# Transposing the second heads' probabilities on the vector engine, with an exchange through DRAM

## The chip, the core and the metric

The kernel runs on one core of a Trainium2 chip. Such a core has a tensor engine (PE) for matrix products and transposes, a vector engine (DVE), a scalar engine (ACT), GpSimd (POOL), and SyncE (SP), which here issues the DMA transfers. The engines run beside each other and wait for each other by semaphores. The measure is device time in microseconds, the median of several runs; lower is better. Times inside the kernel come from one profiled execution.

## The reference

For each of 8 batches and 8 heads, 576 queries attend to 576 keys of 64 numbers. Only the 32 largest scores of a row count. A low-rank mixer over the sequence and a two-layer MLP follow. All is in 32-bit floats.

```python
scores = scale * np.matmul(q, k.transpose(0, 1, 3, 2))          # (8, 8, 576, 576)
kth = np.partition(scores, -32, axis=-1)[..., -32:-31]
scores = np.where(scores >= kth, scores, -1e9)
attn = np.exp(scores - np.max(scores, axis=-1, keepdims=True))
attn = attn / (np.sum(attn, axis=-1, keepdims=True) + 1e-09)
x = np.matmul(attn, v)                                           # heads side by side: (8, 576, 512)
h = x.transpose(0, 2, 1) @ U @ V                                 # rank 32, over the sequence
u = x + h.transpose(0, 2, 1)
out = u + np.maximum(u @ w_ch1, 0.0) @ w_ch2                     # 512 -> 2048 -> 512
```

## The kernel before

Two heads of one batch form a *group*: 32 groups in all, four to a batch. A group has five *steps* (`CH = NT + 1`): t = 0 to 3 take 128 queries of both heads each, t = 4 takes the last 64 queries of both heads in one tile of 128 rows. So there are 160 steps, numbered n = 5 g + t, and the 31st is step 30, the first of group 6. The products of a step are spread over several turns of the main loop: in turn n the scores of step n + 1 are computed, the largest 32 of step n are found, step n - 1 is weighted (masked and put through the exponential), and the values of step n - 2 are taken.

The selection is DVE work: four rounds of MAX8, which finds the 8 largest of a row, with MATCH_REPLACE8 between them, which strikes them out. `front` is a generator, and each `yield` ends a piece that the main loop places among other work. Of a two-head step, head 1 is masked on POOL (`pooled`), head 0 on ACT and POOL (`gaps`):

```python
    def front(g, t):

        if t == 0:
            dens[g] = small.tile([P, 2 * NT + 1], F32, tag="den", name="den", bufs=3)
        chunks, den = S2s.pop((g, t)), dens[g]
        n = len(chunks)
        E2 = attn.tile([P, 2 * S], F32, tag="E", name="E", bufs=3)
        Es = [E2[:, c * S : (c + 1) * S] for c in range(n)]
        sums = [den[:, 2 * t + c : 2 * t + c + 1] for c in range(n)]
        probs[g, t] = E2
        curs, ms = list(chunks), [None] * n
        first = small.tile([P, 2, 8], F32, tag="first", name="first", bufs=3)
        nmax = small.tile([P, 2], F32, tag="nmax", name="nmax", bufs=4)
        order = (1, 0) if n == 2 else (0,)
        for c in order:
            ms[c] = first[:, c]
            nc.vector.max(ms[c], curs[c])
        yield
        early, pooled, gaps = ways(g, t)
        for i in range(1, TOPK // 8):
            if i == 1:
                nc.scalar.mul(nmax[:, 0:n], first[:, 0:n, 0], -SCALE)
                for c in early:
                    weigh(chunks[c], Es[c], nmax[:, c : c + 1])
            for c in order:
                nxt = attn.tile([P, S], F32, tag="rr", name="rr", bufs=3)
                nc.vector.match_replace(nxt, ms[c], curs[c], NEG)
                curs[c] = nxt
            for c in order:
                ms[c] = small.tile([P, 8], F32, tag="m8", name="m8", bufs=8)
                nc.vector.max(ms[c], curs[c])
            yield
        for c in pooled:
            nc.gpsimd.tensor_scalar(Es[c], chunks[c], ms[c][:, 7:8], NEG, ALU.is_lt, ALU.mult)
            nc.gpsimd.tensor_tensor(chunks[c], chunks[c], Es[c], ALU.add)
        for c in early:
            nc.vector.scalar_tensor_tensor(
                out=Es[c],
                in0=chunks[c],
                scalar=ms[c][:, 7:8],
                in1=Es[c],
                op0=ALU.is_ge,
                op1=ALU.mult,
                accum_out=sums[c],
            )
        if t == NT:
            del qkTs[g]
        yield
        for c in gaps:
            least = small.tile([P, 1], F32, tag="least", name="least", bufs=3)
            nc.scalar.mul(least, ms[c][:, 7:8], WIDEN)
            nc.scalar.activation(Es[c], chunks[c], AF.Relu, bias=least, scale=-WIDEN)
            nc.gpsimd.tensor_tensor(chunks[c], chunks[c], Es[c], ALU.subtract)
            yield
        for c in order:
            if c not in early:
                weigh(chunks[c], Es[c], nmax[:, c : c + 1], sums[c])
        if t == NT and g != NPAIR - 1:
            nc.scalar.activation(den, den, AF.Identity, bias=eps)
        yield
```

The probabilities have queries along the partitions; the product with v needs keys there. `turns` does this on the PE, four transposes of 128x128 into one PSUM tile and one ACT copy for each head, and one transpose for the last 64 keys of both heads. `values` multiplies with v:

```python
    def turns(g, t):


        E2 = probs.pop((g, t))
        nh = 2 if t < NT else 1
        PT = attn.tile([P, 2 * NT + 1, P], F32, tag="PT", name="PT")
        PTs[g, t] = PT
        for h in range(nh):
            tp = ps_t.tile([P, NT, P], F32, tag="tp", name="tp")
            for j in range(NT):
                a = h * (S + TAIL) + j * P
                nc.tensor.transpose(tp[:, j, :], E2[:, a : a + P], ident)
            nc.scalar.copy(PT[:, NT * h : NT * h + NT], tp)
            yield
        tp = ps_t.tile([P, P], F32, tag="tp", name="tp")
        a = MAIN if nh == 2 else S - P
        nc.tensor.transpose(tp, E2[:, a : a + P], ident)
        nc.scalar.copy(PT[:, NT * nh], tp)
        yield

# in values(g, t), for a step of two heads:
        PT = PTs.pop((g, t))
        # ... cut
        nc.tensor.matmul(O, lhsT=vd, rhs=PT[:, 2 * NT], start=True, stop=False)
        for j in range(NT):
            for h in range(2):
                nc.tensor.matmul(
                    O[half(h)],
                    lhsT=va[:, h, j, :],
                    rhs=PT[:, NT * h + j],
                    start=False,
                    stop=(j == NT - 1),
                )
```

From group 5 on (`blocked`) the DVE already transposes one thing in 32x32 blocks: q and k of the next group, which small transfers load as blocks into the places where they will be needed. It is one instruction a group, in the turn of t = 1, after the selection:

```python
        if blocked(g):
            nc.vector.transpose(qkT.rearrange("p i n -> p (i n)"), raw.pop(g))
            yield
            return
```

The MLP of a batch runs as filler: `fill()` emits a measured amount of its matmuls between the pieces of the attention of the next batch. The amount is reduced (`EARLY`) up to turn 42, and cut for t = 4 (`SHORT`). The MLP of the last batch has no attention beside it. Its results have channels along the partitions, and `turned_back` transposes them for the output:

```python
    def turned_back(b, chunks, lo, c, oT):


        def run():
            tp = ps_t.tile([P, 3, P], F32, tag="tp", name="tp")
            for i, t in enumerate(chunks):
                n = rows(t)
                nc.tensor.transpose(tp[0:n, i, :], oT[:, OFF[t] - lo : OFF[t] - lo + n], ident)
            ob = mlpp.tile([P, 3, P], F32, tag="ob", name="ob", bufs=3)
            nc.scalar.copy(ob[:, 0:2], tp[:, 0:2, :])
            if NT in chunks:
                nc.scalar.copy(ob[0:TAIL, 2], tp[0:TAIL, 2, :])
            t, cs = chunks[0], slice(c * P, (c + 1) * P)
            nc.sync.dma_start(
                out[b, 0:MAIN, cs].rearrange("(p t) c -> p t c", t=NT)[:, t : t + 2, :],
                ob[:, 0:2],
            )
            if NT in chunks:
                nc.sync.dma_start(out[b, MAIN:S, cs], ob[0:TAIL, 2])

        return run
```

The body of the main loop from group 4 on. The order of PE, ACT, DVE and POOL instructions is the order in which they are written here; the transfers on SyncE are ordered by the compiler's scheduler.

```python
        ease = eased(*divmod(n - 1, CH))
# ... cut: the turns up to 19
        if ease:
            next(last, None)
        fill()
        next(turning, None)
        fill()
        next(turning, None)
        fill()
        next(turning, None)
        fill()
        if ease:
            next(last, None)
        if n - 2 >= ALONE:
            values(*divmod(n - 2, CH))
        if n + 1 < STEPS:
            scores(*divmod(n + 1, CH))
        next(here, None)
        next_params(1)
        if n - 2 >= ALONE and (n - 2) % CH == NT:
            mixing.append(mixed((n - 2) // CH, 5))
        fill()
        next(here, None)
        fill()
        if n <= STEPS:
            turning = turns(*divmod(n - 1, CH))
        fill()
        next(here, None)
        next(ready, None)
        if t in (1, 3):
            next_params(1)
        next(here, None)
        fill()
    while mixing or fillers:
        fill()
```

Of the kernel before, what the change touches and what calls it, by code (L numbers as in the profile page):

```python
# [8 lines left out]
F32 = mybir.dt.float32  # L9
# [17 lines left out]
def kernel(  # L27
# [28 lines left out]
    nc = tc.nc  # L56
    B, H, S, D = q.shape
# [8 lines left out]
    assert S == MAIN + TAIL and D == 64 and H % 2 == 0 and C == 512 and TOPK % 8 == 0  # L66
    NPAIR = H // 2
    NP = B * NPAIR
    SCALE = 1.0 / float(D) ** 0.5
    NV = 3  # L70

# [7 lines left out]
    attn = ctx.enter_context(tc.tile_pool(name="attn", bufs=2))  # L79
    small = ctx.enter_context(tc.tile_pool(name="small", bufs=8))  # L80
    mlpp = ctx.enter_context(tc.tile_pool(name="mlpp", bufs=2))
    ps_s = ctx.enter_context(tc.tile_pool(name="ps_s", bufs=2, space=bass.MemoryType.PSUM))
    ps_t = ctx.enter_context(tc.tile_pool(name="ps_t", bufs=2, space=bass.MemoryType.PSUM))
    ps_m = ctx.enter_context(tc.tile_pool(name="ps_m", bufs=2, space=bass.MemoryType.PSUM))
# [36 lines left out]
    def rows(t):  # L121
        return P if t < NT else TAIL
# [221 lines left out]
    def weigh(chunk, E, nmax, total=None):  # L344

        nc.scalar.activation(E, chunk, AF.Exp, bias=nmax, scale=SCALE, accum_out=total)  # L346

# [13 lines left out]
# [54 lines that stand above are left out]
            nc.scalar.activation(Es[c], chunks[c], AF.Relu, bias=least, scale=-WIDEN)  # L415
            nc.gpsimd.tensor_tensor(chunks[c], chunks[c], Es[c], ALU.subtract)  # L416
            yield
        for c in order:
            if c not in early:
                weigh(chunks[c], Es[c], nmax[:, c : c + 1], sums[c])  # L420
        if t == NT and g != NPAIR - 1:
            nc.scalar.activation(den, den, AF.Identity, bias=eps)
        yield

    def turns(g, t):


        E2 = probs.pop((g, t))
        nh = 2 if t < NT else 1
        PT = attn.tile([P, 2 * NT + 1, P], F32, tag="PT", name="PT")  # L430
        PTs[g, t] = PT
        for h in range(nh):
            tp = ps_t.tile([P, NT, P], F32, tag="tp", name="tp")
            for j in range(NT):
                a = h * (S + TAIL) + j * P
# [8 lines that stand above are left out]
# [7 lines left out]
    def values(g, t):  # L451

        PT = PTs.pop((g, t))
        va, vd, vt = (a[g % NV] for a in (vas, vds, vts))
        O = ps_t.tile([P, P], F32, tag="tp", name="O")
        if t == NT:
            den, x = dens[g], xs[g % 2]
            inverse(g, 2 * NT if g == NPAIR - 1 else 0, 2 * NT + 1)
            for j in range(NT + 1):
                nc.tensor.matmul(  # L460
                    O,
                    lhsT=PT[:, j],
                    rhs=va[:, :, j, :] if j < NT else vt,
                    start=(j == 0),
                    stop=(j == NT),
                )
            for h in range(2):
                nc.scalar.mul(x[half(h), NT, half(h)], O[half(h), half(h)], den[half(h), 2 * NT :])
            return
        nc.tensor.matmul(O, lhsT=vd, rhs=PT[:, 2 * NT], start=True, stop=False)  # L470
        for j in range(NT):
            for h in range(2):
                nc.tensor.matmul(  # L473
                    O[half(h)],
                    lhsT=va[:, h, j, :],
                    rhs=PT[:, NT * h + j],
                    start=False,
                    stop=(j == NT - 1),
                )
        if t == 0:  # L480
            XTs[g] = attn.tile([P, MAIN], F32, tag="XT", name="XT")
        nc.scalar.copy(XTs[g][:, cols(t)], O)  # L482
# [99 lines left out]
    def turned_back(b, chunks, lo, c, oT):  # L582


        def run():
            tp = ps_t.tile([P, 3, P], F32, tag="tp", name="tp")
            for i, t in enumerate(chunks):
                n = rows(t)
                nc.tensor.transpose(tp[0:n, i, :], oT[:, OFF[t] - lo : OFF[t] - lo + n], ident)  # L589
            ob = mlpp.tile([P, 3, P], F32, tag="ob", name="ob", bufs=3)  # L590
            nc.scalar.copy(ob[:, 0:2], tp[:, 0:2, :])
            if NT in chunks:
                nc.scalar.copy(ob[0:TAIL, 2], tp[0:TAIL, 2, :])
            t, cs = chunks[0], slice(c * P, (c + 1) * P)
            nc.sync.dma_start(
                out[b, 0:MAIN, cs].rearrange("(p t) c -> p t c", t=NT)[:, t : t + 2, :],
                ob[:, 0:2],
# [5 lines that stand above are left out]
# [1 line left out]
    MLP_WORK = 2 * NF * NC * S / C  # L604


    CH = NT + 1
    STEPS = NP * CH
    ALONE = NPAIR * CH


    SLOTS, SHORT, EARLY = 8, 0.65, 0.91
# [31 lines left out]
    for n in range(STEPS + 2):  # L644
# [44 lines left out]
        if n < ALONE:  # L689
# [3 lines that stand above are left out]
            if n >= 3:  # L693
                values(*divmod(n - 3, CH))
                if (n - 3) % CH == NT:
                    mixing.append(mixed((n - 3) // CH, 3))
            list(turning)
            fill()
            next(here)
            if t < NT:  # L700
# [3 lines that stand above are left out]
            next(here)  # L704
            next(last, None)
            fill()
            next(here)
            if t in (0, 1):
                next_params(1)
            next(here)  # L710
            fill()
            if n >= 1:
                turning = turns(*divmod(n - 1, CH))
            continue
        if ease:
            next(last, None)
        fill()
        next(turning, None)
        fill()
        next(turning, None)  # L720
        fill()
        next(turning, None)
        fill()
# [9 lines left out]
            mixing.append(mixed((n - 2) // CH, 5))  # L733
        fill()
        next(here, None)
        fill()
        if n <= STEPS:
            turning = turns(*divmod(n - 1, CH))
# [40 lines left out]
```

## Time and profile before

| what | value |
|---|---|
| time, median of 3 | 1819.66 us (1819.0 to 1819.68) |
| span of the profiled execution | 1816.5 us |
| PE busy, share of the span | 1715.5 us, 94% |
| DVE busy | 1498.8 us, 83% |
| ACT busy | 1084.2 us, 60% |
| POOL busy | 846.8 us, 47% |
| chain of work that ended last | PE 81%, DVE 14% |

Busy time is the time in which an engine executes an instruction, whether or not anything waits for it. The chain is followed back from the last instruction, at each step to what released it. A group of instructions is written as line, engine, operation, output and input tile, shapes and count; then busy time and mean time of one in ns; then the idle time of its engine just before, and who ended it. For matmuls the end is modelled and overlaps the next one, so that the distance between two starts, the pitch, is what one costs.

### The profile page before, as it was taken

How to read it: one execution, taken by the hardware profiler on the slowest of the kernel's cores; microseconds unless marked ns; L12 is line 12 of the kernel's file. 1: busy time of each engine (PE TensorE's matmuls, PEld its weight loads, DVE VectorE, ACT ScalarE, POOL GpSimd, SP SyncE). 2: the span in 40 equal slices, each digit the busy share in tenths (PEclk: the TensorE clock that was granted, in tenths of full speed). 3: DMA queues.
4: the chain of work that ended last, by engine and by line, in shares of the span. 5: the costliest groups of instructions: out<-in, count | busy, mean ns of one | idle time of the engine just before them, and what ended most of it. 6: DMA issues, size and time to landing. Idle time of an engine off the chain costs nothing.

```text
span 1816.5 us, 28753 instructions
## 1 busy us (share of the span) xinstructions
PE 1715.5 (94%) x10285; PEld 1293.7 (71%) x10285; DVE 1498.8 (83%) x2995; ACT 1084.2 (60%) x2797; POOL 846.8 (47%) x591
## 2 busy tenths in 40 slices
PE   4666889999999999999999999999999999999999
PEld 2444556787777877788777877788777877788677
DVE  7999998998898888988888889889888898884000
ACT  4777786666656566565666665565656656564111
POOL 4777577444444545535444444444344453543000
PEclk7688899999999999999999999999999999999999
DMA  3232231111100111111001111110011111000000
GB/s 100 79 90 85 68 89 47 32 21 33 21 22 22 21 27 21 32 25 30 17 20 25 24 30 21 32 25 22 19 18 31 21 33 21 8 8 7 6 15 12
DMA packets 193823, 58.21 MB, mean 32 GB/s; under 512 B 156432, under 2 KB 191504, under 8 KB 193680
## 3 DMA queue, kind: packets, MB, share of 16 engines
q1 hardware_dynamic: 192624, 56.11, 13.4%
q8 instruction: 81, 1.33, 0.3%
q14 instruction: 62, 0.51, 0.1%
q10 hardware_dynamic: 1056, 0.26, 0.1%
HBM read 46.89 MB, written 9.44 MB: 31 GB/s over the span
## 4 chain that ended last, share of the span: by engine, by line
PE 81%; DVE 14%; POOL 2%; ACT 1%; issue 1%; DMA 0%; SPq 0%; POOLq 0%; DVEq 0%; ACTq 0%
PE mm L542 26%; PE mm L561 26%; PE sc L328 7%; DVE rr L390 6%; PE O L473 6%; PE tp L436 6%; DVE m L394 5%; DVE first L380 2%; PE sc L315 2%; PE O L460 2%; PE O L470 2%; PE up L517 1%; PE tp L589 1%; PE up L519 1%; PE tp L494 1%
## 5 line engine op out<-in xcount | busy, mean ns | idle before, releaser
L394 DVE MAX8 m<-rr 128x8 f32<-128x576 f32 x864 | 614.9, 749 | 5.5
L561 PE MATMUL mm<-hT,w 128*128 128x256 f32 (+1 forms) x2048 | 555.7, 410 | 0.0
L542 PE MATMUL mm<-uT,w 128*128 128x256 f32 (+1 forms) x2048 | 546.1, 410 | 0.8 <-ACT hT L554 0.8
L542 PEld LDWEIGHTS mm<-uT,w 128*128 128x128 f32 x2048 | 368.3, 190 | 110.7 <-issue 25.6
L561 PEld LDWEIGHTS mm<-hT,w 128*128 128x128 f32 x2048 | 364.4, 190 | 101.2 <-issue 22.5
L397 POOL TENSOR_SCALAR E<-Ssb,m 128x576 f32<-128x576 f32 x127 | 280.8, 2211 | 329.7 <-DVE m L394 249.4
L390 DVE MATCH_REPLACE8 rr<-m,rr 128x576 f32<-128x576 f32 x576 | 427.9, 743 | 0.0
L380 DVE MAX8 first<-Ssb 128x8 f32<-128x576 f32 x288 | 204.1, 745 | 134.3 <-ACT Ssb L341 129.0
L416 POOL TENSOR_TENSOR Ssb<-Ssb,E 128x576 f32<-128x576 f32 x159 | 224.7, 1413 | 192.2 <-ACT E L415 190.8
L437 ACT COPY PT<-tp 128x512 f32<-128x512 f32 x288 | 167.6, 586 | 125.3 <-PE tp L436 123.6
L346 ACT ACTIVATE E<-Ssb,nmax 128x576 f32<-128x576 f32 x288 | 221.0, 771 | 29.6 <-POOL Ssb L398 22.6
L554 ACT ACTIVATE hT<-mm 128x320 f32<-128x320 f32 (+1 forms) x256 | 105.4, 412 | 208.1 <-PE mm L542 208.1
L436 PE MATMUL tp<-ident,E 128*128 128x128 f32 x1152 | 177.7, 279 | 37.9 <-ACT XT L482 15.3
L390 DVE MATCH_REPLACE8 rr<-first,Ssb 128x576 f32<-128x576 f32 x288 | 211.9, 743 | 0.0
L436 PEld LDWEIGHTS tp<-ident,E 128*128 128x128 f32 x1152 | 143.5, 143 | 86.2 <-ACT XT L482 17.1
L398 POOL TENSOR_TENSOR Ssb<-Ssb,E 128x576 f32<-128x576 f32 x127 | 178.9, 1409 | 10.6
L328 PE MATMUL sc<-qkT 64*128 64x288 f32 x1024 | 169.2, 451 | 6.7 <-ACT Ssb L339 5.8
L473 PE MATMUL O<-PT,va 128*64 128x128 f32 x2048 | 143.7, 284 | 0.0
L415 ACT ACTIVATE E<-Ssb,least 128x576 f32<-128x576 f32 x159 | 123.3, 776 | 5.2
L328 PEld LDWEIGHTS sc<-qkT 64*128 64x128 f32 x1024 | 92.6, 196 | 44.8 <-issue 16.2
L473 PEld LDWEIGHTS O<-PT,va 128*64 128x64 f32 x2048 | 112.3, 139 | 16.0 <-issue 1.1
L574 DVE TENSOR_TENSOR oT<-uT,mm 128x320 f32<-128x320 f32 (+1 forms) x8 | 3.6, 454 | 143.2 <-PE mm L561 143.2
(79 smaller groups left out, 1507.6 us busy)
## 6 DMA issues: line engine op xcount, KB each, us to landing
raw<-in_moe_w_ch_dram SPq DMA_DIRECT2D x32, 512.0 KB, 3.8
va<-in_v_dram SPq DMA_DIRECT2D x64, 128.0 KB, 2.1
out_dram<-ob SPq DMA_DIRECT2D x64, 128.0 KB, 1.9
ld<-in_q_dram SPq DMA_DIRECT2D x108, 64.0 KB, 2.4
ld<-in_k_dram SPq DMA_DIRECT2D x108, 64.0 KB, 2.3
ld<-in_q_dram SPq DMA_DIRECT2D x108, 8.0 KB, 2.0
ld<-in_k_dram SPq DMA_DIRECT2D x108, 8.0 KB, 2.0
ld<-in_q_dram SPq DMA_DIRECT2D x9, 128.0 KB, 2.7
```

Source lines behind the costliest of these rows:

```text
L328: nc.tensor.matmul(sc[:, h, 0:HALF], lhsT=qkT[half(h), 0, cols(t)], rhs=qkT[half(h), 1, i * HALF : (i + 1) * HALF], start=True, stop=True,)
L346: nc.scalar.activation(E, chunk, AF.Exp, bias=nmax, scale=SCALE, accum_out=total)
L380: nc.vector.max(ms[c], curs[c])
L390: nc.vector.match_replace(nxt, ms[c], curs[c], NEG)
L394: nc.vector.max(ms[c], curs[c])
L397: nc.gpsimd.tensor_scalar(Es[c], chunks[c], ms[c][:, 7:8], NEG, ALU.is_lt, ALU.mult)
L398: nc.gpsimd.tensor_tensor(chunks[c], chunks[c], Es[c], ALU.add)
L416: nc.gpsimd.tensor_tensor(chunks[c], chunks[c], Es[c], ALU.subtract)
L436: nc.tensor.transpose(tp[:, j, :], E2[:, a : a + P], ident)
L473: nc.tensor.matmul(O[half(h)], lhsT=va[:, h, j, :], rhs=PT[:, NT * h + j], start=False, stop=(j == NT - 1),)
L542: nc.tensor.matmul(ph[:, 0:w], lhsT=w1[:, cc, f * P : (f + 1) * P], rhs=uT[:, cc, lo:hi], start=(cc == 0), stop=(cc == NC - 1),)
L561: nc.tensor.matmul(po[:, 0:w], lhsT=w2[:, f, c * P : (c + 1) * P], rhs=hTs[f][:, 0:w], start=(f == 0), stop=(f == NF - 1),)
```

## The change

From step 30 on (`ROUNDED`), head 1 of each two-head step goes another way. The DVE transposes the 128x512 probabilities in blocks of 32x32, which leaves each block in its own band of 32 partitions. Four transfers write the four bands to a DRAM tile, and one reads it back so that each partition has its key's row. The columns of the result then lie in another order, and the product with v reads them by a pattern (`PB`). Head 0 and the last 64 keys stay on the PE. For this, head 1's exponential is computed before head 0's (`ahead`). The aim is to take work off the PE.

The MLP results of the last batch, except the very last block, are likewise transposed on the DVE in 32x32 blocks, and small transfers put the blocks where they belong in the output. The output buffers `ob` are two in place of three.

```diff
+    ALONE = NPAIR * CH
+    ROUNDED = ALONE + 2 * CH
...
+    dram = ctx.enter_context(tc.tile_pool(name="dram", bufs=2, space=bass.MemoryType.DRAM))
... in front
+        ahead = pooled if shared(g, t) else ()
+        for c in ahead:
+            weigh(chunks[c], Es[c], nmax[:, c : c + 1], sums[c])
+            yield
         for c in order:
-            if c not in early:
+            if c not in early and c not in ahead:
                 weigh(chunks[c], Es[c], nmax[:, c : c + 1], sums[c])
...
+    def shared(g, t):
+        return t < NT and g * CH + t >= ROUNDED
+
+    def blocks(g, t):
+        E2 = probs[g, t]
+        PT = attn.tile([P, 2 * NT + 1, P], F32, tag="PT", name="PT")
+        PTs[g, t] = PT
+        y = attn.tile([P, 4, NT, BLK], F32, tag="y", name="y", bufs=1)
+        nc.vector.transpose(
+            y.rearrange("p r c j -> p c r j"),
+            E2[:, S + TAIL : 2 * S].rearrange("p (c r j) -> p c r j", c=NT, r=4),
+        )
+        away = dram.tile([P, 4, P], F32, tag="away", name="away")
+        for a in range(4):
+            nc.sync.dma_start(
+                away[:, a].rearrange("(r i) n -> i r n", r=4),
+                y[a * BLK : (a + 1) * BLK].rearrange("i r c j -> i r (c j)"),
+            )
+        nc.sync.dma_start(
+            PT[:, NT : 2 * NT].rearrange("p a n -> p (a n)"), away.rearrange("p a n -> p (a n)")
+        )
... in turns
-        for h in range(nh):
+        for h in range(1 if shared(g, t) else nh):
... in values
+        PB = PT[:, NT : 2 * NT].rearrange("p a (c j) -> p c a j", c=NT) if shared(g, t) else None
...
-                    rhs=PT[:, NT * h + j],
+                    rhs=PB[:, j] if h and shared(g, t) else PT[:, NT * h + j],
... in turned_back
+            if b == B - 1 and (lo, c) != (SPAN[1][0], NC - 1):
+                w = sum(rows(t) for t in chunks)
+                ob = mlpp.tile([P, 3 * P], F32, tag="ob", name="ob", bufs=2)
+                nc.vector.transpose(ob[:, 0:w], oT[:, 0:w])
+                for a in range(4):
+                    cs = slice(c * P + a * BLK, c * P + (a + 1) * BLK)
+                    ba = ob[a * BLK : (a + 1) * BLK]
+                    for t in chunks[0:2]:
+                        nc.sync.dma_start(
+                            out[b, 0:MAIN, cs].rearrange("(m i t) c -> t i m c", i=BLK, t=NT)[t],
+                            ba[:, OFF[t] - lo : OFF[t] - lo + P].rearrange("i (m c) -> i m c", c=BLK),
+                        )
+                    if NT in chunks:
...
+                return
... in the main loop
+        away = n <= STEPS and shared(*divmod(n - 1, CH))
         if ease:
             next(last, None)
         fill()
         next(turning, None)
         fill()
         next(turning, None)
+        if away:
+            next(last)
         fill()
...
         fill()
         next(here, None)
+        if away:
+            blocks(*divmod(n - 1, CH))
         fill()
```

More of the change, by code (lines that the diff above doesn't have):

```diff
@@ L68 @@
     NP = B * NPAIR
+    CH = NT + 1
+    ALONE = NPAIR * CH
+    ROUNDED = ALONE + 2 * CH
     SCALE = 1.0 / float(D) ** 0.5
@@ L429, in turns @@
         nh = 2 if t < NT else 1
-        PT = attn.tile([P, 2 * NT + 1, P], F32, tag="PT", name="PT")
-        PTs[g, t] = PT
-        for h in range(nh):
+        if shared(g, t):
+            PT = PTs[g, t]
+        else:
+            PT = attn.tile([P, 2 * NT + 1, P], F32, tag="PT", name="PT")
+            PTs[g, t] = PT
+        for h in range(1 if shared(g, t) else nh):
             tp = ps_t.tile([P, NT, P], F32, tag="tp", name="tp")
@@ L585, in run @@
         def run():
+            cs = slice(c * P, (c + 1) * P)
+            if b == B - 1 and (lo, c) != (SPAN[1][0], NC - 1):
[11 more added lines that the diff above has]
+                    if NT in chunks:
+                        nc.sync.dma_start(
+                            out[b, MAIN:S, cs].rearrange("(m i) c -> i m c", i=BLK),
+                            ba[:, 2 * P : 2 * P + TAIL].rearrange("i (m c) -> i m c", c=BLK),
+                        )
+                return
             tp = ps_t.tile([P, 3, P], F32, tag="tp", name="tp")
@@ L589, in run @@
                 nc.tensor.transpose(tp[0:n, i, :], oT[:, OFF[t] - lo : OFF[t] - lo + n], ident)
-            ob = mlpp.tile([P, 3, P], F32, tag="ob", name="ob", bufs=3)
+            ob = mlpp.tile([P, 3, P], F32, tag="ob", name="ob", bufs=2)
             nc.scalar.copy(ob[:, 0:2], tp[:, 0:2, :])
@@ L593, in run @@
                 nc.scalar.copy(ob[0:TAIL, 2], tp[0:TAIL, 2, :])
-            t, cs = chunks[0], slice(c * P, (c + 1) * P)
+            t = chunks[0]
             nc.sync.dma_start(
@@ L604 @@
     MLP_WORK = 2 * NF * NC * S / C
-    CH = NT + 1
     STEPS = NP * CH
-    ALONE = NPAIR * CH
     SLOTS, SHORT, EARLY = 8, 0.65, 0.91
```

## The prediction

> **What bounds the kernel now.** I read the stretches first. The attention repeats every 20 steps (four groups of five steps), so I cut the span at equal points of that pattern. The columns are PE, PEld, DVE, ACT and POOL busy time with instruction counts, the granted clock, the DMA share and GB/s.
>
> ```profile
> 445.07:653.03 207.96, 207.84 (x1281) 158.72 (x1282) 185.18 (x368) 127.90 (x337) 95.66 (x65) 1.00 0.12 24
> 653.03:860.81 207.78, 207.66 (x1282) 158.54 (x1281) 185.20 (x368) 127.81 (x337) 95.98 (x65) 1.00 0.12 24
> 860.81:1068.58 207.77, 207.65 (x1281) 158.53 (x1281) 185.21 (x368) 127.80 (x337) 95.99 (x65) 1.00 0.12 24
> ...
> 1690.00:1816.50 126.50, 122.61 (x518) 96.02 (x516) 3.63 (x8) 16.30 (x43) 0.00 (x0) 1.00 0.04 10
> ```
>
> In each 207.8 us the PE has 0.1 us of idle time; the DVE is 89% busy, everything else far less. The groups of instructions in that stretch say what the DVE waits for, and give the durations I use:
>
> ```profile
> L380 DVE MAX8 first<-Ssb 128x8 f32<-128x576 f32 x36 | 25.5, 745 | 20.4 <-ACT Ssb L341 19.5 <-ACT Ssb L322 0.8
> ...
> L285 DVE STREAM_TRANSPOSE qkT<-ld 128x1152 f32<-128x1152 f32 x4 | 5.4, 1358 | 0.0
> ```
>
> ```profile
> L437 ACT COPY PT<-tp 128x512 f32<-128x512 f32 x36 | 21.1, 585 | 18.2 <-PE tp L436 18.0
> ```
>
> Of the DVE's idle time 20.4 us is waiting for scores, which the saturated PE delivers late. So the PE sets the pace, with the DVE close behind. A busy PE is not yet a cost, because matmul records overlap; the PE's order of time gives the pitch:
>
> ```profile
> 875.04 0.60 PE L436 MATMUL tp<-ident,E 128*128 128x128 f32 x4
> 875.48 0.70 PE L542 MATMUL mm<-uT,w 128*128 128x320 f32 x2
> 876.02 0.60 PE L436 MATMUL tp<-ident,E 128*128 128x128 f32 x4
> 876.46 0.70 PE L542 MATMUL mm<-uT,w 128*128 128x320 f32 x2
> ```
>
> Four transposes hold the PE from 875.04 to 875.48: **0.44 us**, not 4 x 0.279 us as the mean duration would say.
>
> **What the Trainium skill says.** "VectorE: DVE Perf Modes", section on the three transpose paths, says that the DVE transposes only 32x32 blocks within its banks. This is why the change needs an exchange; no row of this profile shows the limit itself, but L285 shows the price, 1.18 ns per column here. "DMA: Bandwidth & Descriptors", section "Anatomy of one DMA", puts about 2 us of fixed time on a DMA, mostly completion. The trace agrees: 8 KB loads land in 2.0 us, 128 KB of va in 2.1. The same page, "Two DMAs through the same engine are not ordered", says that a DMA reading what another wrote has to wait for its completion, so the two transfers of an exchange cannot overlap. "Perfetto Trace Analysis", section "Identifying the Most-Contended Engine", warns that matmul busy time is a poor measure; here, pitch shows that the PE really is full.
>
> **Part 1, removed from the PE.** From step 30 (group 6) to the end there are 26 groups with four two-head steps each, 104 steps. Each loses the four transposes of its second head, 0.44 us. A group takes 207.77 / 4 = 51.94 us; it loses 4 x 0.44 = 1.76 and would be **50.2 us** if the PE stayed full. ACT loses a 585 ns copy per step, which was on no path.
>
> **Part 2, added to the DVE.** One transpose of 512 columns per step. Between 1358 x 512 / 1152 = 604 ns and somewhat more for a fixed part, I take 0.63 us. The DVE's own work per group is (207.77 - 20.4) / 4 = 46.8 us; plus 4 x 0.63 it is **49.4 us**. That fits under 50.2, but a group has five unequal steps, and only about 1 us of slack is left.
>
> **Part 3, the exchange.** Four DMAs of 64 KB write to DRAM, one of 256 KB reads back. From this profile: SyncE spends 0.41 us (L595) to 0.60 us (L240) on issuing one, so the fourth starts 1.5 to 1.8 us after the transpose; it lands 1.9 to 2.3 us later (out and ld rows); the read lands between the 2.1 us of a 128 KB va and the 3.8 us of a 512 KB w load, say 2.7. With some 0.3 us of semaphores the sum is **about 7 us** (estimate). Bandwidth is no matter: 4 x 512 KB per group is 2 MB in 50 us, 40 GB/s beside 24.
>
> Is it hidden? The DVE's order of time in the old kernel gives the pieces. Step t1 starts at 891.06, t2 at 902.31, t3 could start at 912.26 (it began at 913.00 after 0.74 of idle time): t1 and t2 last 21.2 us. The new transpose comes after the third round of a step, which in step t0 ends at 888.16, 7.0 us after the 881.15 at which that step starts. The loop is then: t1 and t2 with two new transposes 22.5; rounds and transpose in t3 7.6; exchange 7; products with v 1.0, then scores for the next group's t0; from these to the DVE's start 2.1 (879.07 to 881.15); step t0 9.9. In all 43.1 + 7 = **50.1 us**. Three limits thus lie within a microsecond: PE 50.2, loop 50.1, DVE 49.4. With nothing to absorb irregular steps I expect the real period a little above the largest, **50.6 us**.
>
> **Part 4, groups where it cannot pay.** In the first groups after step 30 the filling MLP work is thinned (EARLY). Their DVE starts are 315.34, 363.17 and 412.59: groups of 47.8 and 49.4 us, with hardly a DVE wait inside. With 2.5 us more DVE work they take about 49.4 and 50: a loss of some 2 us.
>
> **Part 5, the tail.** Seven of the eight last result blocks lose their PE transposes: four of three and three of two. The PE stream shows three taking 1743.62 - 1743.29 = 0.33 us; two take 0.22. The sum is 4 x 0.33 + 3 x 0.22 = 1.9 us, all on the PE's path, since the PE is 122.61 of 126.50 us busy there. The eight or twelve small DMAs that replace two are issued while the next block of 7 us or more computes, and the very last block is left as it was.
>
> **Sum.** 24 groups x (51.94 - 50.6) = 32.2; minus 2 for the early groups; plus 1.9 for the tail: 32 us less than 1819.66, about **1788 us**.
>
> **Rivals.** (a) The PE stays full: 24 x 1.74 = 41.8, so about 1778 us. For it: the DVE's waits are long enough to take all new work, and exactly the step after each group's one-head step has the longest wait (3.94 us). (b) The exchange is slower than I think, 9 us: SyncE issues in order, and its loads of q and k (16 small ones at 0.6 us each per group) now stand between the exchange's own transfers. The loop becomes 52.1 us and the change gains nothing or costs a little: 1815 to 1825. For it: the margin is tiny. Against it: loads can be issued during the 2 us in which the writes land. (c) The DVE becomes the bound with waits on top: it needs the second head's exponential 7 us into the next step, in the one-head step already after 4.2 us, while POOL needs 2.2 + 1.4 and ACT 0.77 + 0.19 us for it. A wait of about 0.5 us in that step each group is likely, in others not; some 51 us a group, 1797 us in all. (d) The 4x4x32 pattern makes the transpose twice as slow, 1.2 us: the DVE needs 51.6 us a group and the time is about 1811 us.
>
> **Range and chances.** The best case is about 1778, and a little better only if pitches shrink elsewhere. Most of (b), (c) and (d) end below 1812. I take 1772 to 1810. Faster by over 2% means below 1783, so near the full-PE case: 0.32. Slower by over 2% means above 1856, which needs a new stall of 3 us or more in every group: 0.05. The rest, 0.63, is within 2%.
>
> **What would show it.** Right: a period of 20 steps of 201 to 204 us; the PE with 1 to 3 us idle in it, the DVE over 95% busy, its wait for scores below 5 us; the new transpose at 0.60 to 0.68 us; about 7 us from its end to the landing of the read. Wrong: products with v waiting for a DMA by more than 1 us per group (then (b)); DVE idle time before the new transpose, released by ACT (then (c)); a transpose of 1 us or more (then (d)); or a PE with no idle time and a period near 200.8 (then (a)).

## The result, and the profile after

The changed kernel takes **1775.65 us** (median of 4, 1771.49 to 1776.71) against 1819.33 us, a ratio of 0.976 with a 95% interval of 0.974 to 0.977: 2.4% faster. The prediction was 1788 us, with 1772 to 1810 as its range.

First the stretches of the kernel after, cut at equal points of its pattern of 20 steps (columns as before), and the last stretch, in which only the last MLP is left:

```profile
618.01:818.61 200.60, 200.43 (x1218) 152.87 (x1217) 194.07 (x384) 119.98 (x322) 95.94 (x64) 1.00 0.30 67
818.61:1018.74 200.13, 200.01 (x1218) 152.70 (x1217) 194.04 (x385) 120.06 (x322) 95.95 (x64) 1.00 0.29 67
1018.74:1218.86 200.12, 200.00 (x1218) 152.68 (x1217) 194.06 (x385) 120.07 (x322) 95.96 (x64) 1.00 0.30 67
1647.10:1773.60 126.50, 122.70 (x507) 95.78 (x506) 7.02 (x15) 13.52 (x33) 0.00 (x0) 0.99 0.06 10
```

The period is 200.1 us in place of 207.8, and the PE still has only 0.1 us of idle time in it. The DVE has gone from 89% to 97%. So the bound has not moved; it has become shorter. The groups of DVE instructions from 818.61 to 1018.74:

```profile
L385 DVE MAX8 first<-Ssb 128x8 f32<-128x576 f32 x37 | 26.1, 742 | 3.6 <-ACT Ssb L346 3.6
L446 DVE STREAM_TRANSPOSE y<-E 128x512 f32<-128x512 f32 x16 | 11.2, 698 | 1.1 <-ACT E L351 0.7
...
L290 DVE STREAM_TRANSPOSE qkT<-ld 128x1152 f32<-128x1152 f32 x4 | 5.4, 1360 | 0.0
```

The DVE's wait for scores fell from 20.4 to 3.6 us: the new transposes took the place of idle time. They wait 1.1 us in all for the exponential. On the PE, one piece of four transposes is left in a step, and the products follow sooner:

```profile
863.81 0.60 PE L474 MATMUL tp<-ident,E 128*128 128x128 f32 x4
864.25 0.70 PE L581 MATMUL mm<-uT,w 128*128 128x320 f32 x2
864.79 0.27 PE L479 MATMUL tp<-ident,E 128*128 128x128 f32 x1
```

The exchange's transfers, size and time from issue to landing:

```profile
away<-y SPq DMA_DIRECT2D x416, 64.0 KB, 1.8
PT<-away SPq DMA_DIRECT2D x104, 256.0 KB, 2.8
```

From the starts of the DVE's first round in each step one can date the steps of every kernel. The table, from the profiled executions, is used all through what follows; the column of 20 steps is the range of the five periods between step 40 and step 140.

| kernel | us, median | steps 30 to 40 | 20 steps | start of step 159 to the end |
|---|---|---|---|---|
| before | 1819.33 | 97.25 | 207.77 to 208.09 | 166.5 |
| changed | 1775.65 | 101.68 | 200.12 to 200.60 | 162.3 |
| changed, again | 1775.48 | 101.78 | 200.12 to 200.56 | 162.3 |
| from step 40 | 1772.88 | 97.25 | 200.12 to 200.95 | 162.8 |
| from step 40, again | 1772.36 | 97.25 | 200.12 to 200.99 | 162.9 |
| without the tail | 1777.73 | 101.73 | 200.12 to 200.78 | 164.4 |
| tail only | 1816.18 | 97.24 | 206.52 to 207.78 | 164.4 |
| added work only | 1837.82 | 101.81 | 209.52 to 210.69 | 164.5 |
| added work only, exponential later | 1816.67 | 99.22 | 205.98 to 207.78 | 163.7 |
| removed work only | 1766.36 | 95.65 | 199.50 to 200.12 | 162.9 |
| transpose twice | 1829.13 | 106.44 | 208.10 to 209.13 | 161.5 |
| transpose one round later | 1823.81 | 105.16 | 207.00 to 210.54 | 163.6 |
| one more transfer | 1911.75 | 109.81 | 220.21 to 224.00 | 163.9 |
| two more transfers | 2066.14 | 126.24 | 243.58 to 247.35 | 169.9 |

### The profile page after: what moved, and what is told of

Read it like the earlier page. It is cut to its first block, busy times and chain, and to the rows that moved or that the text cites. A ratio compares the mean times of both kernels' runs of the same rounds, so it can differ in the third digit from the quotient of the medians.

```text
span 1773.6 us, 28992 instructions
## 1 busy us (share of the span) xinstructions
PE 1669.3 (94%) x9851; PEld 1257.5 (71%) x9851; DVE 1560.3 (88%) x3106; ACT 1029.4 (58%) x2682; POOL 846.8 (48%) x591
## 4 chain that ended last, share of the span: by engine, by line
PE 75%; DVE 16%; POOL 4%; ACT 3%; issue 2%; DMA 1%; SPq 0%; POOLq 0%; DVEq 0%
PE mm L581 25%; PE mm L600 24%; DVE rr L395 7%; PE sc L333 6%; PE O L512 6%; DVE m L399 6%; PE tp L474 3%; DVE first L385 2%; PE sc L320 2%; PE O L498 2%; PE up L556 1%; PE O L508 1%; POOL E L402 1%; PE up L558 1%; PE tp L648 1%
## 5 line engine op out<-in xcount | busy, mean ns | idle before, releaser
L600 PE MATMUL mm<-hT,w 128*128 128x256 f32 (+1 forms) x2048 | 547.4, 410 | 0.0
L600 PEld LDWEIGHTS mm<-hT,w 128*128 128x128 f32 x2048 | 368.3, 190 | 106.8 <-issue 22.5
L351 ACT ACTIVATE E<-Ssb,nmax 128x576 f32<-128x576 f32 x288 | 223.3, 776 | 52.4 <-POOL Ssb L403 34.9
L474 PE MATMUL tp<-ident,E 128*128 128x128 f32 x736 | 116.0, 283 | 37.1 <-ACT XT L521 14.6
L474 PEld LDWEIGHTS tp<-ident,E 128*128 128x128 f32 x736 | 92.1, 145 | 68.7 <-ACT XT L521 16.6
L475 ACT COPY PT<-tp 128x512 f32<-128x512 f32 x184 | 106.6, 585 | 49.0 <-PE tp L474 46.4
```

The source lines that it names most:

```text
L600: nc.tensor.matmul(po[:, 0:w], lhsT=w2[:, f, c * P : (c + 1) * P], rhs=hTs[f][:, 0:w], start=(f == 0), stop=(f == NF - 1),)
```

## The experiments

**Added work only.** Everything the change adds is done, but the PE transposes both heads as before, and what the exchange brings back lands in `y` and is not used.

```diff
-            PT[:, NT : 2 * NT].rearrange("p a n -> p (a n)"), away.rearrange("p a n -> p (a n)")
+            y.rearrange("p r c j -> p (r c j)"), away.rearrange("p a n -> p (a n)")
... in turns
-        for h in range(1 if shared(g, t) else nh):
+        for h in range(nh):
... in values
-                    rhs=PB[:, j] if h and shared(g, t) else PT[:, NT * h + j],
+                    rhs=PT[:, NT * h + j],
```

> All that the change adds to DVE and DMA in the attention is done (the transposes, the four writes, the read, the earlier exponential), but what is read back goes into the tile y again and is not used: the PE transposes both heads as before. If the PE sets the pace and the additions are hidden, the time stays near the kernel before, with up to 5 us more in the first groups, 1.9 us less in the tail: 1817 to 1823 us. If the 104 transposes of 0.694 us were on the path they would show as 72 us more, 1890 us; if the saving came from something else than PE time (the earlier exponential, for one), the time would be well below 1810 us.

It took 1837.8 us (ratio 1.010, 1.009 to 1.012): none of the cases expected. Of the PE's waits from 310 to 1670 us by far the longest is this one:

```profile
PE O L503 <- ACT PT L475: 14.2, 27, 1.6
```

L475 copies the transposes of the last 64 keys, and L503 is the first product of `values`. In this kernel, where head 1 has a piece of `turns` again, the early exponential (L351) stood ahead of that copy in ACT's order:

```profile
887.99 0.78 ACT L351 ACTIVATE E<-Ssb,nmax 128x576 f32<-128x576 f32 x1
888.66 0.19 ACT L351 ACTIVATION_READ_ACCUMULATOR E<-Ssb,nmax 128x1 f32 x1
888.76 0.25 ACT L475 COPY PT<-tp 128x128 f32<-128x128 f32 x1
```

```profile
889.06 0.49 PE L503 MATMUL O<-PT,vd 128*128 128x128 f32 x2 [0.40 <-ACT PT L475]
```

The transpose was ready at 888.1 and the copy came 0.7 us later. So this run had a fault of its own. I repeated it with the exponential one piece later.

```diff
-        if away:
-            next(last)
         fill()
         next(turning, None)
+        if away:
+            next(last)
```

> As the run with the added work only (1837.8 us), but the early exponential of head 1 is put after the third piece of the transposes in place of the second. In that run the PE waited 14 us for the copy of the last 64 keys' transposes, which stood behind this exponential on ACT. My theory: the added DVE and DMA work is hidden once that wait is gone, 1817 to 1824 us. Rival: DVE and exchange are themselves on the path of the PE-bound kernel, then it stays at 1835 us or more.

1816.67 us, as fast as the tail alone (1816.18), with the old period of 207.77 us, although the DVE does 104 more transposes and the exchange runs all along:

```profile
829.75:1037.52 207.77, 207.65 (x1282) 158.53 (x1281) 194.75 (x385) 128.34 (x338) 96.05 (x64) 1.00 0.28 65
```

**In the steady part the additions cost nothing.** The two runs also show that the place of one exponential in ACT's order was worth 21 us; the wait shown is 14.2 of them.

**Removed work only.** The other half: the PE leaves out head 1's transposes and nothing takes their place. Products for head 1 read head 0's probabilities, so head 1's result is not computed.

```diff
-        if away:
-            blocks(*divmod(n - 1, CH))
... in values
-                    rhs=PB[:, j] if h and shared(g, t) else PT[:, NT * h + j],
+                    rhs=PT[:, j] if h and shared(g, t) else PT[:, NT * h + j],
```

> Only what the change removes: from step 30 the PE leaves out the transposes of head 1, and nothing is put in their place. No DVE transpose, no exchange; the products for head 1 read head 0's transposed probabilities, so head 1's result is not computed. This is the price of the removed PE work alone. If the additions cost time only in the two first groups (4.4 us), it takes 1771 to 1772 us; the period of 20 steps is the changed kernel's 200.1 us. Rival: the additions cost something all along, so the period is shorter than 200.1 us and the time 1766 us or less.

1766.36 us, lower than I expected, but the period is 200.12 us, the changed kernel's:

```profile
812.07:1012.19 200.12, 200.00 (x1218) 152.68 (x1217) 185.02 (x368) 119.66 (x322) 95.92 (x64) 1.00 0.12 25
```

The rival is wrong about the steady part, I about the start: in the profiled executions of this kernel and of the changed one beside it, 1767.0 and 1774.5 us, 6.1 of the 7.5 us between them lie in steps 30 to 40 (95.65 and 101.78). I had taken it that the removal saves nothing there; it saves 1.6 us of the old kernel's 97.25, all in group 7 (steps 35 to 39). In the old kernel the PE was full in that group; the second line is the removed-only kernel:

```profile
363.17:412.59 49.42, 49.40 (x321) 39.83 (x320) 46.16 (x93) 32.04 (x84) 23.12 (x15) 1.00 0.11 22
364.64:412.45 47.81, 47.07 (x304) 38.03 (x303) 46.14 (x92) 28.77 (x80) 23.12 (x15) 1.00 0.12 23
```

**Where it begins.** One line: the new way from step 40 on.

```diff
-    ROUNDED = ALONE + 2 * CH
+    ROUNDED = ALONE + 4 * CH
```

> The new way begins at step 40 in place of 30, so groups 6 and 7 are as in the old kernel. My theory: these two groups are bound by the DVE in the old kernel, and in the changed one they cost 4.4 us more (54.2 to 102.2 us longer is not it: from step 30 to 40 the trace has 97.25 us before and 101.68 after), partly because the PE waits for the exchange at 363 us and its granted clock then falls to half until about 369 us. So from step 40 should be about 4 us faster than the changed kernel: 1771 to 1772 us. Rival: the saving is the same 0.44 us of PE time for each step, whatever the place; then 8 steps fewer make it 3.5 us slower, 1779 us.

(The 54.2 and 102.2 us in this expectation are wrong: steps 30 to 40 take 97.25 us before and 101.68 after. And only group 6 is as long without the PE's transposes, 47.8 us; group 7 was bound by the PE, as shown above.) It took 1772.88 us. As this is close to the changed kernel's time, both were run again side by side on one chip.

> The changed kernel as it is, on the same chip as the next run. 1775 us; where a run has no stall of the PE near 363 us, 1771 us.

> The run that begins at step 40, again, beside the changed kernel. My theory: 2 to 4 us faster than the changed kernel. The rival that each step saves its 0.44 us everywhere has it 3.5 us slower.

1775.48 us (1774.37 to 1776.28) against 1772.36 (1771.71 to 1772.39): 3.1 us apart, and the runs do not overlap. Their ratios to the kernel before are 0.9768 (0.9754 to 0.9783) and 0.9750 (0.9736 to 0.9765). The rival is wrong: eight steps *fewer* with the new way are faster. Beginning at step 40 is thus the best version here that computes everything.

**The tail.** Once the change without it (the condition in `turned_back` made False), once it alone (`ROUNDED = NP * CH`).

> The change without its part for the last result: the last batch's blocks go over the PE as before. My theory: the tail is worth the PE transposes it removes, 1.9 us, so 1777.5 us. Rival: it is worth nothing since the output transfers end at the same time, 1775.6 us; or it costs time by its 77 small transfers, below 1775 us.

> Only the last result is changed; all probabilities go over the PE as before. My theory: 1.9 us less than the kernel before, 1817.4 us. The rival that the tail is worth nothing has 1819.3 us.

1777.73 us, 2.1 more than the changed kernel, and 1816.18 us, where the kernel before had 1818.45 beside it (ratio 0.9989, 0.9982 to 0.9995). The stretch from step 159 to the end is 2.1 us shorter with the tail's change than without it, in both pairs. (The small transfers number 72, not 77.)

**How much room the DVE has.** Each transpose is written twice.

```diff
+        nc.vector.transpose(
+            y.rearrange("p r c j -> p c r j"),
+            E2[:, S + TAIL : 2 * S].rearrange("p (c r j) -> p c r j", c=NT, r=4),
+        )
```

> The DVE makes each of its 104 transposes twice (the same result is written again), 0.69 us each. The DVE's work without waits is 195.8 us in a period of 200.1, 48.95 us a group; with 4 x 0.69 it is 51.7, so the DVE is the bound: 1.7 us x 24 and some 5 us in the first two groups, about 1820 us. Rival: the PE is the bound and the DVE has slack, 1776 to 1780 us.

1829.13 us, 9 more than I expected. The period became 208.1, and its stretch and the DVE's wait for scores show why:

```profile
838.91:1047.03 208.12, 203.08 (x1217) 153.10 (x1216) 205.06 (x402) 119.02 (x320) 95.97 (x64) 1.00 0.28 65
```

```profile
L385 DVE MAX8 first<-Ssb 128x8 f32<-128x576 f32 x37 | 26.1, 740 | 0.0
```

No wait for scores is left on the DVE, while the PE has 5.0 us of idle time: the DVE is the bound, at 52.0 us a group. The changed kernel had about 1.1 us of room in a group of 50.0.

**How much room the exchange has.** First the transpose is moved one round of the selection later, with the same work.

```diff
-        if away:
-            blocks(*divmod(n - 1, CH))
         fill()
         if n <= STEPS:
             turning = turns(*divmod(n - 1, CH))
         fill()
         next(here, None)
+        if away:
+            blocks(*divmod(n - 1, CH))
```

> The changed kernel with the DVE's transpose placed one round of the selection later: the same work, but 2.9 us later in a two-head step and 1.7 us later in the one-head step. The exchange's transfers are unchanged, and on SyncE each read back still comes ahead of the next step's writes. Loop theory: 48.7 + 2.9 = 51.6 us a group against the period of 50.0, so 24 x 1.6 = 38 us and a few more in the first groups, 1815 to 1820 us, with the PE waiting for the read back. Since a stall of the PE may halve its granted clock for some microseconds, as in the one stall of the changed kernel, it may be more, up to 1860 us. Rival: the exchange has more slack than my sum says; 1776 to 1785 us.

1823.81 us. Four of the five periods are 207.0 to 207.9 us, 51.8 us a group, where the expectation has 51.6; the fifth, 210.5 us, has a longer stall of 2.5 us and then half the granted clock. The wait is the one expected: the product with v for head 1, after head 0's first, stands for the read back.

```profile
925.62 1.09 PE L512 MATMUL O<-PT,va 128*64 128x128 f32 x14 [0.51 <-DMA PT<-away]
935.95 1.09 PE L512 MATMUL O<-PT,va 128*64 128x128 f32 x14 [1.41 <-DMA PT<-away]
```

Then one or two more transfers in the chain:

```diff
+        more = dram.tile([P, 4, P], F32, tag="more0", name="more0")
+        nc.sync.dma_start(more.rearrange("p a n -> p (a n)"), away.rearrange("p a n -> p (a n)"))
+        away = more
```

> The changed kernel with one more transfer of 256 KB in the exchange, DRAM to DRAM, which adds some 3 us to it. My loop sum with what the trace after shows: t1 and t2 22.3, rounds and transpose of t3 7.7, exchange 5.7, products 1.0, scores to DVE 2.1, t0 9.9: 48.7 us, 1.3 below the period of 50.0. With 3 us more it is 51.7, 1.7 us over, and 24 such groups give 41 us: about 1815 us. Rival: the exchange has buffers enough to be late by 3 us without anybody waiting; then 1776 us.

> Two more transfers in the exchange, some 6 us. Loop theory: 54.7 us a group, 4.7 over, about 1890 us, and the PE waits for the read back. Rival of free buffers: 1776 us, or far less than twice the effect of one transfer.

1911.75 and 2066.14 us: the direction is right, the size far off. With one more transfer the group takes about 55.5 us, not 51.7; with two it takes 60.9 to 61.8, not 54.7. For one more transfer, SyncE's order of time shows what was added; this is from the last step of a group, SyncE first and then the PE:

```profile
912.34 0.54 SPq L457 DMA_DIRECT2D more<-away  x1
...
918.24 0.32 SPq L452 DMA_DIRECT2D away<-y  x1
918.65 0.38 SPq L459 DMA_DIRECT2D PT<-more  x1
```

```profile
917.63 0.43 PE L515 MATMUL O<-PT,va 128*64 128x128 f32 x2
921.57 1.25 PE L515 MATMUL O<-PT,va 128*64 128x128 f32 x14 [3.51 <-DMA PT<-more]
922.75 2.29 PE L333 MATMUL sc<-qkT 64*128 64x288 f32 x8
```

The added copy was issued at 912.34 and landed at 915.2. But the scheduler had put the first write of the *next* step's exchange ahead of the last read in SyncE's order, and that write waited for a DVE transpose that ended at 918.2. So the read left at 918.65 and the PE stood for 3.5 us. Then the scores took 2.29 us in place of 1.24; the granted clock was 0.59 and 0.56 in the 4 us from 922. The run does not test the loop sum cleanly; it shows what follows when the room is used up. In the run with two more transfers the PE waits 139 us for the read back between 400 and 1600 us, against 74 with one; whether the same order lengthens it is not shown.

## Why the prediction held, and where it did not

**The bound and the PE's saving (part 1): right.** The pitch of 0.44 us for four transposes gave 50.2 us a group; measured are 200.12 / 4 = 50.03. The removed-only kernel has the same period, so the 0.15 us more belongs to the PE. Part of it is probably that the first product of `values` no longer waits for the 64-key copy on ACT: the kernel before had five such waits in each period, for instance 0.39 us from 877.65 to 878.04 where 0.31 is usual; that is 0.4 of the 0.6 us in a period. No run isolates it.

**The DVE's addition (part 2): right.** 0.63 us was estimated. The transpose lasts 0.69 us, but the next instruction starts 0.62 us after it:

```profile
835.59 0.69 DVE L446 STREAM_TRANSPOSE y<-E 128x512 f32<-128x512 f32 x1
836.21 0.05 DVE L395 MATCH_VALUE_LOAD rr<-m,rr 128x8 f32 x1
```

Without its waits the DVE needs (200.13 - 3.6 - 1.1) / 4 = 48.9 us a group, against 49.4 predicted.

**The exchange (part 3): about 1 us too long.** In a step t3, the one in the loop, the transpose was done at 858.52, the read was issued at 861.84, and with 2.8 us to land it arrived at 864.6: 6.1 us, not 7; in the one-head step after it the read was issued as soon (866.87 and 870.13). The writes landed after 1.8 us where I took 1.9 to 2.3, and the four issues follow each other at 0.44 us. In the step t1 of this group it was 7.8 us, since a load of q, which waits for the DVE, stands ahead of the read on SyncE, and in its t2 some 7.5 (848.03, 852.73); these are not in the loop. With t1 and t2 at 22.3 us and the rounds and transpose of t3 at 7.7, the loop sum is 22.3 + 7.7 + 6.1 + 1.0 + 2.1 + 9.9 = 49.1 us in place of 50.1. (The 48.7 in the expectations above took 5.7 us for the exchange, a misreading of mine.) With one round more (2.9 us) it is 52.0; the late-transpose run has 51.8, and so supports the sum.

**The step that failed: the choice of 50.6 us.** I put 0.4 us on the largest of three limits because nothing seemed left "to absorb irregular steps". There is nothing irregular: the pattern repeats every four groups, the limits do not add, and with 1.1 us of room on the DVE and 0.9 in the loop the PE ran at its own limit. 24 x (50.6 - 50.03) = 13.7 us, slightly more than the 12.4 by which 1788 missed; the errors in the other parts nearly cancel, which is luck. Rival (a), the full PE at 1778 us, was the right one: the sign named for it, no idle time on the PE and a period near 200.8 us, is what the profile shows (0.1 and 200.1). In the steady part (b), (c) and (d) were not realised, although doubling the transpose makes the DVE the bound, and delaying it by a round the loop. The margin was thin all the same: one more round of delay, or one more transfer, cost the whole gain.

**The early groups (part 4): right for the DVE, but a stall was missed.** Predicted was a loss of 2 us, from groups of 49.4 and 50; measured are 4.4 between steps 30 and 40. The added-only kernel with the later exponential takes 49.61 us for each of the two groups and loses 2.0 us, the DVE's part. That there was hardly a DVE wait inside was misread, though: the waits before 363.17 and 412.59 are 1.1 and 2.7 us. In the changed kernel group 7 takes 49.61 us too, but group 6 52.07. This rest comes with a stall of the PE in the last step of group 6, which I had not seen coming:

```profile
360.43 0.49 PE L508 MATMUL O<-PT,vd 128*128 128x128 f32 x2 [1.02 <-ACT PT L480]
360.85 0.43 PE L512 MATMUL O<-PT,va 128*64 128x128 f32 x2
363.00 1.97 PE L512 MATMUL O<-PT,va 128*64 128x128 f32 x14 [1.72 <-DMA PT<-away]
364.90 2.29 PE L333 MATMUL sc<-qkT 64*128 64x288 f32 x8
```

```profile
360.00:362.00 2.00, 0.85 (x4) 0.49 (x4) 1.83 (x5) 0.43 (x3) 1.92 (x3) 1.00 0.56 75
362.00:364.00 2.00, 1.00 (x10) 1.00 (x12) 1.88 (x4) 1.77 (x5) 1.28 (x1) 0.61 0.27 100
364.00:366.00 2.00, 2.00 (x12) 1.41 (x10) 1.02 (x2) 0.45 (x3) 0.00 (x0) 0.50 0.16 35
366.00:368.00 2.00, 2.00 (x8) 1.13 (x5) 0.03 (x1) 1.40 (x4) 0.00 (x0) 0.50 0.45 100
368.00:370.00 2.00, 2.00 (x8) 1.63 (x8) 2.00 (x4) 0.29 (x2) 0.00 (x0) 0.69 0.37 130
```

The PE stands for 1.0 and 1.7 us. The granted clock (third column from the right) falls to half in the second wait, at about 362.4, and stays there for some 6.8 us. The scores come late, and the DVE waits 2.9 us for them:

```profile
367.97 1.42 DVE L385 MAX8 first<-Ssb 128x8 f32<-128x576 f32 x2 [2.92 <-ACT Ssb L346]
```

The added-only kernel waits 0.3 us there. About 1 us of the second wait is rival (b) in small: SyncE issued two output transfers between the second and the third write of this exchange, so that the read came back 7.2 us after the transpose (355.81; issued at 360.23, landed at 363.0) and not after 6.1. The profiles of the changed kernel's repetition and of the kernel without the tail show the same stall and the same mean clock of 0.72 from 360 to 372 us. Beginning at step 40 has neither stall nor loss, and gains 3.1 us. How much of the extra loss is the stall and how much the clock is not separated; an order of transfers without the two outputs was not run.

**The tail (part 5): right.** 1.9 us predicted, 2.1 by each of two runs.

**The sum, in the profiled executions.** Before step 30, 0.6 us more; steps 30 to 40, 4.4 more; from step 40 to the start of step 159, 1237.4 us before and 1193.7 after, 43.8 less by the unrounded figures; from there to the end, 4.2 less, half of it the tail. Together 43.0 less, and so are the spans (1816.53 and 1773.56).

## What to carry to other kernels

Here one engine was full and another had waits that the full one caused; work moved between them cost nothing in the steady part until those waits were used up. In such a case, take the saving from the pitch of what is removed, and do not add a margin for several near limits that do not add. Then look for the place where the order of bounds differs (here the first ten steps) and leave it out of the change. The chain over DRAM was hidden only as long as its loop closed within the period, and another transfer ahead of its last link in SyncE's order lengthened it.

## What the runs showed of the hardware

In the changed kernel the granted clock fell to half within the second of two PE gaps of 1.0 and 1.7 us, and stayed there for some 6.8 us; about 6.2 of these lie after the PE had started again, which at half speed is some 3 us of lost work (an estimate). The length of a gap alone does not decide it. The kernel before has a gap of 1.3 us up to 439.27 and then half the clock from about 440.7 to 444.1; in the kernel that begins at step 40 the same gap (from 438.9) is followed by the full clock, and so are single gaps of 1.7 us up to 365.5 and 406.9 in the late-transpose run. In order, before and from step 40:

```profile
440.00:442.00 2.00, 1.83 (x10) 1.51 (x12) 1.97 (x6) 0.93 (x4) 0.00 (x0) 0.68 0.36 89
442.00:444.00 2.00, 2.00 (x18) 1.67 (x16) 1.70 (x3) 1.51 (x5) 0.79 (x1) 0.50 0.26 38
```

```profile
440.00:442.00 2.00, 1.84 (x18) 1.57 (x20) 1.97 (x5) 1.08 (x3) 0.11 (x1) 1.00 0.34 54
442.00:444.00 2.00, 2.00 (x21) 1.32 (x17) 1.97 (x5) 1.39 (x5) 0.00 (x0) 1.00 0.25 71
```

The drop before fits the first period in the table, which is 1.6 us longer in the kernel before (208.09) than in the tail-only one (206.52), where the clock stayed full. What decides it these runs do not show. Four 128x128 transposes of 32-bit data hold the PE 0.44 us back to back, well under half of the 1.1 us that their durations of 279 ns add up to. Plain DVE transposes of 256, 320 and 1152 columns took 0.445, 0.512 and 1.36 us, which puts 512 columns at about 0.71 us; those of 512 columns, written in runs of 32 elements, took 0.694 us, so the pattern cost nothing.
